# Five idle products among TensorE's first work, and a new order of all work, in a delta-rule attention and cosine-gate kernel

## The chip, the cores and the metric

The kernel runs on one core of a Trainium2 chip. A core has five engines with queues of their own: TensorE (PE in the profile; its weight loads are PEld), VectorE (DVE), ScalarE (ACT), GpSimd (POOL) and SyncE (SP, which here only issues DMAs). Each works through its own list of instructions in order, and waits on semaphores for what others make. The metric is the device time of one execution in microseconds (us); lower is better.

## The reference

```python
q, k, v: (4, 8, 768, 48); beta: (4, 8, 768)           # B, H, S, D
k_n = k / (norm(k) + 1e-06)
for t in range(S):
    y[:, :, t] = q_t @ state
    v_old = k_t @ state
    state = state + beta_t * outer(k_t, v_t - v_old)   # delta rule, state 48 x 48 per head
x = y.transpose(0, 2, 1, 3).reshape(3072, 384)
h = x @ w_in                                           # w_in (384, 2048)
out = (h * cos(h)) @ w_out                             # w_out (2048, 384)
```

The weights arrive in 64-bit words and are narrowed on the chip to 32 bits.

## The kernel before

**Attention.** The sequence is cut into 24 units of 32 steps. All 32 pairs of batch and head of a unit are worked at once. For unit n: `turn` (L589) transposes k and q on TensorE through p_t (from unit 8 on VectorE does it, `turn_blocks`), ScalarE copies them out (`turn_out`, L599), `gram` (L620) makes the products of keys with keys and queries in p_g, and VectorE scales them out (`gram_keys` L634, `gram_queries` L743). The unit's lower triangle has to be inverted. Units 0 to 3 do it by halves: TensorE spreads rows (`rows`, L702, p_r), VectorE (units 0 and 1) or GpSimd (2 and 3) eliminates them (`eliminate`, L722 and L729), `unfold` (L737) lays the result out, and three products solve (`solve_half` and `between`, L859, `solve`, L892). Units 4 to 23 are inverted in pairs on GpSimd (`invert`, L792 and L799, in tiles gb and z), with a trip through DRAM on either side (`gram_put` L761, `gram_get` L770, `put` L803, `get` L812 into zt), and then solve (L892). `solve_out` (L902) scales the solution, `update` (L915) and `update_out` (L923, L925) carry the state on, `state` (L829) and `within` (L932) make the output in p_kq, and `features` (L951) transposes it into x.

**Feed-forward.** Two units make a pair p, 256 tokens. Pairs 0 and 1 multiply x by w_in plainly (`hidden`, L975, p_h, 24 instructions a tile); later pairs use a scheme with fewer products of sums of blocks (`x_sum` L1068, `in_sums` L1115, `layer` L1153, `layer_out`). The gate is h cos h by ScalarE and VectorE (L1016, L1023, L1032, L1035). The output of pair 0 is plain (`output`, L1176), that of the others a seven-product scheme (`product`, L1233, p_out; `left` L1249, `right` L1262, `collect` L1285).

**Weights.** 28 loads (`weights`, L484; 12 for w_in, 16 for w_out) go into six stages that are used in turn, and each is narrowed by ScalarE (`split`, L492 and L494), VectorE (`shift`, L498 and L503) and GpSimd (`add`, L507). A load waits until the sixth load before it is added.

**The order.** The kernel adds 2143 tasks with `add`, each with a key, an engine and what it needs. `Order.LINE` is a written list of all task numbers; `Order.run` (its `run` walks that list) emits the tasks in this order, and so fixes each engine's queue. `Order.OTHER` is a set of tasks that go to their second engine: `x_sum` is GpSimd's unless it is listed, then VectorE's; `left` and `right` are VectorE's unless listed, then GpSimd's; `fold` and `unfold` VectorE's unless listed, then ScalarE's. PSUM has one bank pair for "two" (p_t, p_w, p_v, p_u, p_s, p_z and most p_g), one for p_kq, three banks "h" for p_r and p_h, and p_out. `halfpi` is a column of constants that GpSimd sets at the start.

Of the kernel before, what the change touches and what calls it, by code (L numbers as in the profile page):

```python
# [45 lines left out]

class Order:
# [3 lines left out]
        ('weigh', 1, 0), ('fold', 2), ('weigh', 1, 1), ('fold', 3), ('unfold', 2),  # L51
        ('right', 4, 6), ('x_sum', 2, 'd'), ('x_sum', 2, 'n'), ('x_sum', 2, 'm'),
        ('x_sum', 2, 'e'), ('x_sum', 2, 'k'), ('x_sum', 2, 'g'), ('x_sum', 2, 'i'),
        ('x_sum', 2, 'l'), ('x_sum', 2, 'f'), ('x_sum', 2, 'h'), ('x_sum', 2, 'b0'),
        ('left', 2, 4, 0), ('x_sum', 3, 'd'), ('x_sum', 3, 'n'), ('x_sum', 3, 'm'),
        ('x_sum', 3, 'e'), ('x_sum', 3, 'k'), ('x_sum', 3, 'g'), ('x_sum', 3, 'i'),
        ('x_sum', 3, 'l'), ('x_sum', 3, 'f'), ('left', 3, 4, 0), ('x_sum', 4, 'd'),
        ('x_sum', 4, 'n'), ('x_sum', 4, 'm'), ('x_sum', 4, 'e'), ('x_sum', 4, 'k'),
        ('x_sum', 4, 'l'), ('x_sum', 4, 'h'), ('x_sum', 4, 'b0'), ('left', 4, 1, 0),
        ('left', 4, 4, 1), ('left', 4, 3, 1), ('x_sum', 5, 'd'), ('x_sum', 5, 'n'),  # L60
        ('x_sum', 5, 'm'), ('x_sum', 5, 'e'), ('left', 5, 1, 0), ('left', 5, 1, 1),
        ('left', 5, 4, 0), ('left', 5, 3, 0), ('left', 5, 3, 1), ('x_sum', 6, 'd'),
        ('x_sum', 6, 'm'), ('x_sum', 6, 'e'), ('x_sum', 6, 'g'), ('x_sum', 6, 'i'),
        ('x_sum', 6, 'l'), ('x_sum', 6, 'f'), ('x_sum', 6, 'b0'), ('left', 6, 1, 1),
        ('left', 6, 3, 0), ('left', 6, 3, 1), ('x_sum', 7, 'd'), ('x_sum', 7, 'n'),
        ('x_sum', 7, 'm'), ('x_sum', 7, 'e'), ('x_sum', 7, 'g'), ('x_sum', 7, 'i'),
        ('x_sum', 7, 'l'), ('x_sum', 7, 'b0'), ('left', 7, 1, 1), ('left', 7, 4, 0),
        ('left', 7, 3, 0), ('left', 7, 3, 1), ('x_sum', 8, 'd'), ('x_sum', 8, 'm'),
        ('x_sum', 8, 'k'), ('x_sum', 8, 'g'), ('x_sum', 8, 'h'), ('x_sum', 8, 'b0'),
        ('left', 8, 1, 0), ('left', 8, 3, 0), ('x_sum', 9, 'd'), ('x_sum', 9, 'm'),  # L70
        ('x_sum', 9, 'e'), ('x_sum', 9, 'k'), ('x_sum', 9, 'g'), ('x_sum', 9, 'i'),
        ('x_sum', 9, 'l'), ('x_sum', 9, 'f'), ('left', 9, 1, 0), ('left', 9, 4, 0),
        ('left', 9, 4, 1), ('x_sum', 10, 'd'), ('x_sum', 10, 'n'), ('x_sum', 10, 'e'),
        ('x_sum', 10, 'k'), ('x_sum', 10, 'g'), ('x_sum', 10, 'l'), ('x_sum', 10, 'f'),
        ('x_sum', 10, 'h'), ('x_sum', 10, 'b0'), ('left', 10, 1, 1), ('left', 10, 2, 1),
        ('left', 10, 4, 0), ('left', 10, 3, 0), ('x_sum', 11, 'n'), ('x_sum', 11, 'k'),
        ('x_sum', 11, 'l'), ('x_sum', 11, 'f'), ('x_sum', 11, 'h'), ('left', 11, 2, 1),
        ('left', 11, 4, 0), ('left', 11, 4, 1), ('left', 11, 3, 0),
# [3 lines left out]
9 92 2031 0 1 123 15 2035 16 93 17 2 14 3 11 21 54 55 10 18 2039 56 4 124 60 22 23 57 58 19 20 6 95  # L82
24 181 207 61 26 27 62 53 2043 2047 30 96 32 28 126 29 63 36 65 2032 2036 64 127 25 31 34 33 66 39
2033 35 101 97 2040 67 102 73 132 37 68 40 128 2041 38 98 2037 133 69 184 185 129 2034 2042 41 2038
42 43 44 71 2044 2048 70 8 2051 182 45 46 2045 47 2055 48 49 50 2056 190 78 191 2049 72 51 2052 52
94 7 74 2057 125 2059 103 2060 2063 104 75 105 134 2053 135 137 106 186 2046 2061 138 107 59 2050
131 2058 76 208 2064 108 139 2067 77 2071 2054 237 79 136 2075 183 2065 739 2062 140 141 150 142 740
80 144 81 82 99 741 145 100 147 5 83 143 263 293 2079 84 146 148 153 85 151 86 88 87 210 2068 149 89
2076 742 211 2069 743 12 154 2072 152 744 187 90 156 2066 91 745 240 157 155 2077 109 192 158 159
110 746 193 194 241 130 160 2083 2087 238 759 162 2080 2073 212 2084 213 2081 163 747 760 161 2070  # L90
214 761 164 165 749 195 166 748 2085 2088 111 2078 2082 112 2074 242 215 209 750 217 762 2086 751
763 113 114 2089 752 2091 216 2095 769 115 2092 264 2099 2103 753 2093 116 770 774 117 2100 119 771
243 2101 2107 118 764 772 2096 244 218 120 2108 2094 246 219 247 775 2104 167 121 2090 122 773 168
776 779 777 2097 220 2098 169 2102 221 170 171 2111 807 778 2109 222 319 2115 2105 172 13 2106 173
2119 822 808 809 174 2110 810 175 765 239 2123 177 766 811 767 265 823 2112 295 2116 189 768 349
2127 2131 176 178 817 179 824 2113 818 819 180 820 2124 2120 821 812 266 754 2117 825 267 2121 223
2114 197 826 2125 2118 791 813 755 248 2128 756 296 198 2122 2126 814 249 250 780 268 301 2135 2132
757 815 269 270 2139 827 816 251 271 2129 224 2133 225 2136 272 2140 828 273 2137 792 781 795 2130
758 842 837 302 196 829 830 796 831 838 375 321 322 226 2141 832 2134 880 799 878 879 188 2138 297
2142 199 839 200 245 782 201 203 783 840 843 298 202 785 844 800 888 841 274 803 845 204 205 227 786  # L100
833 882 885 303 793 797 206 228 787 275 229 894 883 323 881 834 230 784 358 294 788 835 836 231 405
233 232 846 789 234 276 847 889 848 235 850 351 236 253 851 304 357 277 900 907 853 854 377 320 902
901 804 352 852 849 910 903 911 305 904 278 306 915 916 906 912 324 802 905 325 856 917 919 326 920
884 908 913 914 254 918 858 859 327 279 307 790 860 890 359 886 909 280 300 926 928 861 895 892 921
929 862 281 801 927 930 932 857 329 922 805 923 891 328 864 252 931 933 924 353 893 330 255 934 925
431 936 866 256 806 935 938 798 939 257 887 937 259 958 260 282 378 867 942 940 258 855 896 354 299
959 954 943 283 284 261 946 868 955 262 960 865 956 285 941 869 331 870 944 794 286 961 945 962 379
287 289 290 288 871 948 963 899 291 309 292 897 898 949 360 863 461 957 1013 952 964 332 950 333 872
361 1015 965 1014 953 874 875 1020 407 1024 362 355 947 1016 1028 380 1017 978 1025 966 1018 350 414
1026 876 951 381 873 1029 376 1019 382 1021 967 363 1030 383 434 1027 968 334 969 1032 1031 335 408  # L110
970 1033 983 979 336 1022 982 337 384 308 1034 985 877 971 310 988 1041 1039 989 1023 972 984 1042
1045 980 981 973 991 385 1035 974 1040 1036 1046 413 1043 975 409 311 1049 1037 976 1038 993 1044
312 977 1047 990 386 1048 1050 986 994 313 315 487 433 987 316 338 992 1051 1055 995 1052 314 415
317 339 469 318 1067 1056 1053 340 1071 996 341 1057 997 1054 342 1068 343 1058 356 345 999 346 344
1001 1061 1072 1002 1063 410 1062 435 1003 1004 347 1069 348 1073 998 1126 1065 416 470 387 406 388
517 543 389 390 1066 1059 1005 1070 417 1064 418 1127 1128 436 463 1075 419 1074 411 437 1060 1076
1129 1137 1006 1141 365 464 1007 391 1138 1142 1133 1130 392 1134 1132 471 1131 1009 1077 1145 1139
439 1146 1079 1000 438 1135 366 1078 1080 1143 1154 1010 1011 393 441 1140 1083 1144 440 1136 465
1084 1081 1155 364 1147 1095 367 1158 1085 1082 466 368 1086 1091 490 1008 489 394 1152 1098 1159
1092 1153 1093 369 371 1156 370 442 1094 525 372 1087 1148 432 1157 526 1162 373 1096 1149 1160 1088  # L120
395 1101 1150 1151 1089 374 1161 396 1102 1163 491 1164 397 1168 1104 398 1165 399 401 1106 1090
1097 1169 402 1184 400 546 573 1166 1172 1167 1185 1188 403 443 1170 1099 404 1171 421 472 412 444
1239 1107 1174 1176 1186 445 1100 1173 422 1240 473 474 527 1108 1187 1109 492 493 1192 1105 1177
545 1110 446 1012 1175 462 1112 1114 447 1178 448 1193 1179 1189 1111 1115 495 475 449 1116 1250
1246 1117 1241 1190 1103 1194 1191 1118 1242 1204 1119 1254 1113 1205 494 519 1251 1247 1120 1243
581 1255 1122 496 1206 420 1248 497 1245 520 1256 1258 423 1123 1195 424 425 427 1180 1259 1124 1207
426 1249 1244 1181 428 1252 1209 1253 1257 1267 1182 1200 1268 451 1260 1201 429 1271 1265 1183 452
# [89 lines left out]
def kernel(  # L217
# [32 lines left out]
    nc = tc.nc  # L250
# [1060 lines left out]
    add = order.add  # L1311
# [498 lines left out]
```

## Time and profile before

| | before |
|---|---|
| three runs, median | 650.61 us (649.26 to 652.42) |
| profiled execution, its time | 650.96 us |
| its span, first to last instruction | 648.2 us |
| mean granted TensorE clock | 0.991 |
| busy: PE, PEld, DVE, ACT, POOL | 618.3, 579.9, 501.3, 264.4, 430.7 us |
| DMA | 49.99 MB, mean 77 GB/s |
| instructions | 28202 |

The profile is of one execution. Busy time counts an instruction from its start to its end; matmuls overlap, and their ends are modelled. The row "PEclk" gives the clock that TensorE was granted, as a share of full speed. The chain that ended last is followed back from the last instruction: each piece was released by the one before it. "issue" is time in which an engine waited for nothing that the profile shows.

The order of TensorE's first tasks in the kernel before, with the start of each in us: turn 0 (4.6), turn 1 (8.4), gram 0 (10.5), gram 1 (13.6), rows of unit 0 (14.7 to 21.3), turn 2, rows, turn 3, rows, solve_half 0 (29.3), between 0 (31.5), rows(1,1) (32.9), solve 0 (36.0), update 0 (38.7), within 0 (40.2), turn 4 (41.7), state 1 (43.2), features 0 (47.1), gram 2 (48.5), rows(1,3) (49.6), gram 3 (51.0), hidden(0,0) (52.1), rows, solve_half 1 (58.4), between 1 (60.1), solve 1 (61.7), update 1 (64.6), within 1 (65.5), turn 5 (68.2), hidden(0,2) (69.1).

### The profile page before, as it was taken

Reading aid. Unit: us, or ns where it says so; the run is one execution under the profiler, and the core shown is the slowest. Engines: PE = TensorE matmul, PEld = TensorE weight load, DVE = VectorE, ACT = ScalarE, POOL = GpSimd, SP = SyncE. Lnnn points to the kernel's source line nnn. Section 1 sums busy time; section 2 is a strip of 40 time slices with the busy share of each in tenths; the row PEclk is TensorE's granted clock in tenths of the full one; section 3 lists DMA queues with packets and bytes.
Section 4 is the critical chain, followed back from the end, with each engine's and each line's share of the span. In section 5 each row is a group of like instructions: output and inputs, shape, how many; then the busy total and the mean of one; then the engine's idle time right before and its main releaser. Section 6 shows DMA issues by size and latency. Waiting matters only on the chain.

```text
span 648.2 us, 28202 instructions
## 1 busy us (share of the span) xinstructions
PE 618.3 (95%) x12306; PEld 579.9 (89%) x12306; DVE 501.3 (77%) x967; ACT 264.4 (41%) x466; POOL 430.7 (66%) x772
## 2 busy tenths in 40 slices
PE   4869899999999989999999999999999999999997
PEld 3858888886899979999999999899999999999997
DVE  7986777899989868788788875788677678757671
ACT  4534655722233432442533532543532434345430
POOL 3446788988858788587787687886786685111211
PEclk9997999999999999999999999999999999999999
DMA  8792475554352544554514443504513302000000
GB/s 163 193 238 66 109 185 139 132 98 78 55 104 41 104 73 62 102 70 76 106 34 71 82 73 70 86 10 62 110 17 69 66 2 43 19 3 25 2 25 24
DMA packets 202923, 49.99 MB, mean 77 GB/s; under 512 B 194544, under 2 KB 197760, under 8 KB 202800
## 3 DMA queue, kind: packets, MB, share of 16 engines
q1 hardware_dynamic: 201536, 47.82, 37.5%
q8 instruction: 96, 1.57, 1.0%
q10 hardware_dynamic: 1088, 0.20, 0.2%
q14 instruction: 27, 0.22, 0.1%
q0 software_dynamic: 176, 0.18, 0.1%
HBM read 38.19 MB, written 9.96 MB: 74 GB/s over the span
## 4 chain that ended last, share of the span: by engine, by line
PE 81%; DVE 6%; DMA 5%; issue 3%; POOL 2%; ACT 1%; SPq 1%; ACTq 0%; DVEq 0%; POOLq 0%
PE p_out L1233 27%; PE p_h L1153 26%; PE p_kq L829 4%; PE p_h L975 3%; PE p_s L915 3%; PE p_r L702 3%; PE p_u L892 3%; PE p_g L620 3%; PE p_kq L932 3%; PE p_out L1176 3%; PE p_o L1233 2%; DMA kp<-in_k_dram 1%; DMA z_dr<-z 1%; PE p_z L951 1%; PE p_t L589 1%
## 5 line engine op out<-in xcount | busy, mean ns | idle before, releaser
L792 POOL TENSOR_TENSOR part<-z,gb 128x126 f32<-128x126 f32 (+22 forms) x310 | 139.9, 451 | 34.9 <-DMA gb<-g_dr 12.5
L799 POOL TENSOR_TENSOR z<-z,part 128x126 f32<-128x126 f32 (+22 forms) x310 | 139.3, 449 | 24.3
L1233 PE MATMUL p_out<-w_out,g_ffn 128*128 128x192 f32 x672 | 123.0, 330 | 0.3 <-DVE o L1285 0.3
L1233 PEld LDWEIGHTS p_out<-w_out,g_ffn 128*128 128x128 f32 x672 | 107.7, 190 | 1.9 <-DVE o L1285 0.5
L1032 ACT ACTIVATE turns<-turns,halfpi 128x512 f32<-128x512 f32 x96 | 68.2, 720 | 63.8 <-DVE turns L1023 63.7
L1233 PE MATMUL p_out<-w_sum,g_ffn 128*128 128x192 f32 x496 | 89.2, 328 | 0.0
L1249 POOL TENSOR_TENSOR g_ffn<-g_ffn 128x512 f32<-128x512 f32 x30 | 41.2, 1380 | 70.1 <-DVE g_ffn L1249 29.2
L1153 PE MATMUL p_h<-x_sum,w_in 128*128 128x128 f32 x640 | 84.0, 278 | 1.5 <-ACT p_h L1165 1.2
L1153 PEld LDWEIGHTS p_h<-x_sum,w_in 128*128 128x128 f32 x640 | 78.2, 191 | 3.3 <-ACT p_h L1165 1.4
L1233 PEld LDWEIGHTS p_out<-w_sum,g_ffn 128*128 128x128 f32 x496 | 79.6, 190 | 0.9 <-issue 0.2
L1016 ACT ACTIVATE turns<-g_ffn,quarter_turn 128x512 int32<-128x512 f32 x70 | 50.4, 721 | 58.5 <-DVE g_ffn L1170 29.7
L1170 DVE TENSOR_TENSOR g_ffn<-g_ffn,p_h 128x512 f32<-128x512 f32 x80 | 54.1, 681 | 18.5 <-PE p_h L1153 14.0
L1023 DVE SCALAR_TENSOR_TENSOR turns<-g_ffn,turns 128x512 f32<-128x512 f32 x70 | 52.8, 760 | 11.6 <-ACT turns L1016 11.4
L1035 DVE TENSOR_TENSOR g_ffn<-turns,g_ffn 128x512 f32<-128x512 f32 x70 | 52.7, 758 | 11.1 <-ACT turns L1032 11.1
L1285 DVE SCALAR_TENSOR_TENSOR o<-p_out,o 128x192 f32<-128x192 f32 x74 | 25.2, 353 | 36.4 <-PE p_out L1233 32.8
L1153 PE MATMUL p_h<-x_sum,in_sum 128*128 128x128 f32 x400 | 52.4, 277 | 0.0
L1153 PEld LDWEIGHTS p_h<-x_sum,in_sum 128*128 128x128 f32 x400 | 49.2, 192 | 0.5
L975 PE MATMUL p_h<-x_ffn,w_in 128*128 128x128 f32 x384 | 48.4, 285 | 0.2 <-issue 0.2
L975 PEld LDWEIGHTS p_h<-x_ffn,w_in 128*128 128x128 f32 x384 | 46.2, 199 | 1.3 <-issue 0.5
L1249 DVE TENSOR_TENSOR g_ffn<-g_ffn 128x512 f32<-128x512 f32 x58 | 43.9, 765 | 3.4 <-POOL g_ffn L1249 2.3
L536 POOL TENSOR_TENSOR knrm<-ksum,halves 128x16 f32<-128x16 f32 (+1 forms) x14 | 36.8, 2629 | 13.4 <-DVE ksum L524 13.4
L1165 ACT COPY p_h<-p_h 128x512 f32<-128x512 f32 x40 | 23.0, 576 | 48.7 <-PE p_h L1153 46.3
(144 smaller groups left out, 1058.1 us busy)
## 6 DMA issues: line engine op xcount, KB each, us to landing
gb<-g_dr SPq DMA_DIRECT2D x20, 256.0 KB, 4.4
vp<-in_v_dram SPq DMA_DIRECT2D x96, 48.0 KB, 3.0
in_sum<-in_moe_w_out_dram SPq DMA_DIRECT2D x12, 384.0 KB, 3.7
out_dram<-o SPq DMA_DIRECT2D x23, 192.0 KB, 2.5
in_sum<-in_moe_w_in_dram SPq DMA_DIRECT2D x8, 512.0 KB, 4.2
kp<-in_k_dram SPq DMA_DIRECT2D x128, 24.0 KB, 1.9
z_dr<-z SPq DMA_DIRECT2D x10, 256.0 KB, 3.6
zt<-z_dr SPq DMA_DIRECT2D x80, 32.0 KB, 2.1
```

The source lines that it names most:

```text
L536: nc.gpsimd.tensor_tensor(out=scales[m][2][:, part], in0=sums[m, part.start][:, 0:n], in1=halves[:, 0:n], op=ALU.pow,)
L792: nc.gpsimd.tensor_tensor(out=part, in0=z[:, 0:rows, j, None].to_broadcast(shape), in1=a[:, j, None, j + 1 :].to_broadcast(shape), op=ALU. ...
L799: nc.gpsimd.tensor_tensor(out=behind, in0=behind, in1=part, op=ALU.subtract)
L975: nc.tensor.matmul(p_h[:, i], w_in[:, t, (4 * k + i) * 128 : (4 * k + i + 1) * 128], xts[p][:, t, unit * 128 : (unit + 1) * 128], start=(i ...
L1016: nc.scalar.activation(turns[p, f], hidden_of(p, f), AF.Identity, bias=quarter_turn, scale=TURN)
L1023: nc.vector.scalar_tensor_tensor(out=r, in0=hidden_of(p, f), scalar=TURN, in1=t, op0=ALU.mult, op1=ALU.subtract,)
L1032: nc.scalar.activation(r, r, AF.Sin, bias=halfpi, scale=2.0 * math.pi)
L1035: nc.vector.tensor_tensor(out=place(p, f), in0=step_of(rests.pop((p, f)), f), in1=step_of(hidden_of(p, f), f), op=ALU.mult,)
L1153: nc.tensor.matmul(p_h[:, e], in_block(*w)[:, e], x_of(p, b), start=new and e == 0, stop=True, skip_group_check=True,)
L1170: nc.vector.tensor_tensor(out=part_of(p, to), in0=part_of(p, one), in1=part_of(p, two), op=op)
L1233: nc.tensor.matmul(p_o, left(p, part, a)[:, e % 4], right(e, b), start=(e == 0), stop=(e == FT // 2 - 1), skip_group_check=True,)
L1249: either(("left", p, x, s), nc.vector, nc.gpsimd).tensor_tensor(out=left(p, s, to), in0=left(p, s, one), in1=left(p, s, two), op=op)
```

## The change

Five tasks ("heat", 0) to ("heat", 4) are added to TensorE. Each multiplies a 128 x 128 operand, the constant column `halfpi` repeated 128 times, with the same column repeated 512, 256, 256, 512 or 128 times, into p_out. Nothing reads the result: the first output product of pair 0 starts p_out anew, and is made to come after the five in the written order. The five depend on no other task.

```diff
+HEAT = (512, 256, 256, 512, 128,)
...
+    def heat(width):
+        one = halfpi.to_broadcast([128, 512])
+        nc.tensor.matmul(
+            flat_out[:, 0:width], one[:, 0:128], one[:, 0:width],
+            start=True, stop=True, skip_group_check=True,
+        )
...
                 if last:
                     deps.append(last)
+                else:
+                    deps += [("heat", x) for x in range(len(HEAT))]
...
+    for i, width in enumerate(HEAT):
+        add(("heat", i), "PE", 0.2, lambda width=width: heat(width))
```

`LINE` is written anew, from

```diff
-9 92 2031 0 1 123 15 2035 16 93 17 2 14 3 11 21 54 55 10 18 2039 56 4 124 60 22 23 57 58 19 20 6 95
+92 0 1 2 21 15 3 16 9 54 2143 10 11 17 55 18 93 123 2031 124 2035 14 4 60 56 57 6 22 2039 95 23 61
```

to its end (2143 to 2147 are the five products). Read out as queues, TensorE's first tasks become: turn 0, **heat 0**, turn 1, gram 0, gram 1, rows(0,0), turn 2, rows(0,1), rows(0,2), state 0, rows(0,3), turn 3, rows(1,2), rows(1,0), solve_half 0, between 0, **heat 1**, solve 0, rows(1,1), update 0, within 0, **heat 2**, turn 4, state 1, features 0, rows(1,3), gram 2, **heat 3**, gram 3, hidden(0,0), rows(2,0), solve_half 1, rows(2,1), between 1, rows(2,2), rows(2,4), solve 1, **heat 4**, rows(2,3), update 1, within 1, turn 5, hidden(0,2). State 0 issues no instruction.

VectorE's queue, from the elimination of unit 0 to gram_keys 2, has in both kernels the same tasks but one (spread(0,1) comes later) in another order; sum(2,0) moves behind solve_out 0, and shift 0 and sum(1,1) behind the last elimination of unit 0. On SP the first loads were k 2, weights 0, k 3, weights 1, q 2, v 0, weights 2, q 3, and are now k 2, q 2, k 3, weights 0, q 3, weights 1, v 0, weights 2. On ScalarE turn_out 3 now stands ahead of unfold 0 instead of behind it. On GpSimd eight instead of ten weight adds stand between the first and the last step of the first inverse (units 4 and 5).

`OTHER` gets a new list, from 117 to 120 entries: 22 left sums and 18 x sums go from VectorE to GpSimd, 15 left sums and 14 x sums the other way; one right sum each way; one fold goes to VectorE, and one unfold to ScalarE:

```diff
-        ('weigh', 1, 0), ('fold', 2), ('weigh', 1, 1), ('fold', 3), ('unfold', 2),
-        ('right', 4, 6), ('x_sum', 2, 'd'), ('x_sum', 2, 'n'), ('x_sum', 2, 'm'),
+        ('weigh', 1, 0), ('fold', 2), ('weigh', 1, 1), ('unfold', 2), ('unfold', 3),
+        ('right', 4, 0), ('left', 1, 2, 0), ('x_sum', 2, 'd'), ('x_sum', 2, 'n'),
...
```

## The prediction

> **What bounds the kernel now.** I read the page first, then stretches of the span with their busy time, then the chain that ended last, the timeline of the first 75 us and the waits. All times are from the one profiled execution: span 648.2 us, time 650.96 us, which is 0.35 us above the median of the three times shown (650.61).
>
> The page's first two parts:
>
> ```profile
> PE 618.3 (95%) x12306; PEld 579.9 (89%) x12306; DVE 501.3 (77%) x967; ACT 264.4 (41%) x466; POOL 430.7 (66%) x772
> ...
> PEclk9997999999999999999999999999999999999999
> ```
>
> TensorE is the engine to watch, and the granted clock shows one dip, at 48.6 to 64.8 us. Stretches of 3.4 us around it (columns: PE, PEld, DVE, ACT, POOL busy with counts, granted clock, DMA share, GB/s):
>
> ```profile
> 39.45:42.80 3.35, 3.35 (x93) 3.01 (x87) 2.43 (x6) 1.00 (x3) 2.23 (x3) 1.00 0.85 276
> 42.90:46.20 3.30, 1.33 (x89) 1.03 (x87) 3.02 (x9) 2.63 (x5) 1.84 (x2) 1.00 1.12 302
> 46.30:49.60 3.30, 2.73 (x110) 2.07 (x110) 2.21 (x9) 1.61 (x3) 0.81 (x1) 0.50 0.71 188
> 49.70:53.00 3.30, 3.30 (x75) 3.11 (x75) 2.46 (x6) 0.25 (x1) 1.68 (x2) 0.50 0.05 10
> 53.10:56.40 3.30, 3.30 (x18) 3.30 (x17) 3.20 (x8) 2.06 (x6) 2.34 (x3) 0.50 0.45 161
> 56.60:59.90 3.30, 3.30 (x81) 2.98 (x80) 3.20 (x9) 2.32 (x5) 1.07 (x2) 1.00 0.18 34
> ...
> 68.00:648.20 580.20, 568.10 (x11201) 535.36 (x11201) 448.16 (x821) 235.77 (x409) 396.07 (x731) 1.00 0.36 67
> ```
>
> The last line says that from 68 us on TensorE works 568.1 of 580.2 us at full clock, so little is to be had there. The others say that a stretch with 40% work (42.9 to 46.2) is followed by half clock, and that this ends after a stretch of unbroken streaming (53.1 to 56.4). From the chain, whole run:
>
> ```profile
> 40.30 1.43 PE p_kq L932 x64
> 41.73 1.58 PE p_t L589 x8
> 44.23 2.07 issue
> 49.70 1.38 PE p_r L702 x6
> 52.20 4.95 PE p_h L975 x24
> 57.14 1.31 PE p_r L702 x8
> 66.33 1.60 issue
> 69.23 2.68 PE p_h L975 x24
> ```
>
> The same 24 products p_h take 4.95 us at 52 and 2.68 us at 69. And the clock row misleads before 42.8 us: it says 1.00, but 64 products p_kq take 1.43 us at 40.30 and 62 take 0.81 us at 65.5, and four transposes begin 213 ns apart at 4.6 and about 110 ns apart at 68. So I read half clock from the start to 42.8 us, full to 46.3, half to 56.5, full after. Up to 29 us that costs little: VectorE has 13.05 us of work in the 15.4 us from 12.0 to 27.4, and its elimination of unit 0's rows ends at 27.4. After that VectorE waits for TensorE:
>
> ```profile
> 37.57 1.02 DVE L902 TENSOR_TENSOR u<-p_u,bz 128x384 f32<-128x384 f32 x2 [1.25 <-PE p_u L892]
> ...
> 40.41 0.96 DVE L925 COPY st<-p_s 128x768 f32<-128x768 f32 x1 [0.89 <-PE p_s L915]
> ...
> 49.74 0.42 DVE L634 TENSOR_TENSOR rows<-p_g,bs 128x256 f32<-128x256 f32 x1 [1.03 <-PE p_g L620]
> ```
>
> **The change, part by part.** *The five products.* 512+256+256+512+128 = 1664 columns. No row shows such a product. The nearest, p_out of 192 columns, does four in 1.30 us, 1.69 ns a column: 2.8 us for all five at full clock, 5.6 at half. They wait for nothing but a constant that is there at 0.8 us; what is queued behind them is the next product on TensorE. Places: heat 0 before the second unit's transposes, in front of a 1.94 us wait of p_g (until 13.58) that nothing here ends sooner; heat 1 while VectorE makes solve(0)'s right side; heat 2 ahead of turn(4); heat 3 before gram(3), whose bank VectorE has first to empty; heat 4 (0.2 us) in the 0.59 us wait of update(1). I take 0 for them: each lies before a wait or beside VectorE. Bounds: 0 and 5.6 us, the latter if the waits are gone and the clock is low; less than nothing is the next item.
>
> *The clock.* From solve(0) to heat 3 the new order leaves TensorE about 14 us of work at half clock (1.48+1.96+1.56+1.43+0.85+1.58+1.7+0.84+1.38+1.19, the chain's rows, heats 1 and 2 and the state product by the above) with no wait I can see before VectorE's gram_keys(2). One stretch like 53.1 to 56.4 is in it, so I expect full clock by about 39 us and no fall at 46. What half clock costs on the chain: from 29.3 to 42.8 p_w 0.73, p_v 0.69, p_r 0.98, p_u 0.60, p_s 0.67, p_kq 0.62, p_t 0.55, 4.8 us in all (each row less the same row after 57 us, p_r halved); from 46.3 to 57.1 p_kq 0.37, p_z 0.51, p_g 0.39 and 0.31, p_r 0.69, p_h 2.27, 4.5 us in all. [...]
>
> *The order of the start.* solve(0) now stands ahead of rows(1,1), which held TensorE from 32.9 to 36.0 while its right side was ready at 34.0. VectorE's waits of 1.25 and 0.89 us go: 2.1 us, at either clock. With full clock the 1.03 us go too, then gram(3) starts when its bank is empty instead of behind p_r (0.45) and runs faster (0.31), and the first hidden tile saves 2.27: 4.1 us. Sum at the end of that tile: 6.2 us (2.6 with a low clock). VectorE is late next: its queue has the same work before gram_keys(2) but spread(0,1). On SP two q loads (4 issues, 1.9 us each) pass weights 0 and 1; their first use is a shift that VectorE does after its elimination, at 27.6 or later, so I cost that at 0, at most 1.9.
>
> *The rest.* Relative order hardly differs. 22 left sums and 18 x sums go from VectorE to GpSimd, 15 and 14 come back: net 7 at 1.27 and 4 at 0.46 us, 11 us more GpSimd of 431. What matters is the inverse on GpSimd: solve(6), (8), (12) and (19) start within 0.9 us of their zt's landing. By summed durations solve(6) stands 1.7 us nearer in TensorE work while GpSimd's weight adds before inverse 3 are the same 28: 1.7 us lost there. The 8.4 us of other idle gaps after 68 us I leave as they are; bounds from 3 us better (the 1.57 at 240 and 1.23 at 407 us gone) to the 7 us of the second rival.
>
> Sum: 650.96 - 6.2 + 1.7 = 646.5; against the median, 646.1.
>
> **Rivals.** *1. The clock falls back.* GpSimd and VectorE pace the start, TensorE at full clock finishes its 14 us early, stands before gram_keys(2) and drops to half as at 46.3. For it: 40% work was enough for that. Against: heat 3 fills 0.85 us there, and 7.45 of 10.2 us busy (59.9 to 70.1) kept the clock. Then 2.6 us are gained, heats 2 and 3 lie open at half clock (2.6): 651.
>
> *2. Slower: the inverse chain.* GpSimd is busy 61.3 of 72 us from 58 to 130, partly by adds that wait for weights. If inverse 3 still starts at 140, whatever the start gained ends in waits of solve(6) for zt, and the later pairs follow: from the second gram to the solve, units 16 and 18 come 0.5 and 5.3 us nearer, units 20 and 22 have 6.9 and 3.0 us more GpSimd work inside their inverse; less the present slack of 1.8, 2.3, 1.1 and 2.7 us and 3.9 us more distance at unit 20, that is 3.0+1.9+0.3, and 1.7 at unit 6: 7 us. Time 657.5. It decides where p_u's waits for zt, now 0.7 us in all, pass 6 us. Against: inverse 2 has two adds less inside (2.6 us).
>
> *3. Full clock from 12 us.* Transposes, heat 0, transposes and gram(0) run without a break from 6.8 to 12.3 us, and the clock stays. All 9.4 us and the 2.07 us gap go, less 1.7: 640.8. Against: VectorE's 13.05 of 15.4 us; TensorE busy without a break from 18.9 to 25.8, with transposes and p_r, did not raise the clock. [...] Unbroken work with transposes before 42.8 did end in full clock, so the trace leaves it open.
>
> **Chances.** Forecast 0.45 (643 to 650), rival 1 0.24, rival 2 0.20, rival 3 0.11. A measurement tells about 0.5%, 3.25 us, from no change, so faster means under 647.4 and slower over 653.9: faster 0.49 (three quarters of the forecast's 0.45, rival 3, a little of rival 1), slower 0.20, same 0.31. Range 639.5 to 657.5: rival 3 to rival 2, as both signs are open.
>
> **What would show it.** Right: p_h's first 24 products take about 2.7 us and end near 51; 64 products p_kq of within(0) take under 1 us, or those of within(1) begin at about 59; no clock of 0.5 after 46. Order: solve_out(0) starts at or before 36.5 without a wait. Wrong: p_g of unit 3 still at 51; heats ahead of an idle VectorE; p_u waiting for zt several us; busy TensorE from 68 us to the end below 97%. Where fetch gaps ("issue", 2.07 and 1.60 us) fall in the new order I cannot tell; one more or less moves the time by 2 us.

## The result, and the profile after

The changed kernel takes 644.8 us (median of four runs, 644.34 to 645.68), beside 650.58 us (649.26 to 652.42) for the kernel before on the same chip: a ratio of 0.9911, 95% interval 0.9884 to 0.9937. By the bound of 0.5% that the prediction set it is faster, and the number is near the forecast of 646.1. The way to it is another than the forecast's. The profiled execution took 644.59 us, its span is 642.8 us (before 648.2), its mean clock by the records 0.981 (before 0.991).

The changed kernel's lines stand 5 (at its start) to 13 (from the output products on) lower in the code: `hidden` is L980 for L975, `state` L834 for L829, `rows` L707, `eliminate` L727 and L734, `collect` L1298, the five products L1194.

From its page, the busy times and the clock row:

```profile
PE 613.6 (95%) x12316; PEld 572.7 (89%) x12316; DVE 505.4 (79%) x955; ACT 263.3 (41%) x467; POOL 447.9 (70%) x783
...
PEclk9677999999999999999999999999999999999999
```

The row shows three low slices of 16 us where it showed one. That is not more half clock: the row of before said full up to 42.8 us, where the prediction read half clock from the products' times (64 p_kq in 1.43 us at 40.30, 62 in 0.81 at 65.5), and this one has records from 12.2 us on. The mean clocks can't be compared for the same reason. GpSimd has 17 us more work (the forecast had 11). The same stretches as in the prediction (PE, PEld, DVE, ACT, POOL busy with counts, granted clock, DMA share, GB/s), the last of them to the new end:

```profile
39.45:42.80 3.35, 2.14 (x52) 1.50 (x52) 3.31 (x7) 0.48 (x1) 3.35 (x2) 1.00 0.88 169
42.90:46.20 3.30, 3.26 (x201) 2.90 (x184) 3.09 (x8) 1.48 (x3) 3.30 (x4) 1.00 0.51 94
46.30:49.60 3.30, 1.03 (x2) 0.20 (x2) 3.20 (x6) 0.00 (x0) 2.34 (x3) 1.00 0.81 241
49.70:53.00 3.30, 1.36 (x65) 1.19 (x65) 2.62 (x13) 1.74 (x5) 0.15 (x1) 0.50 0.93 304
53.10:56.40 3.30, 3.30 (x16) 3.30 (x17) 3.27 (x8) 0.85 (x3) 1.59 (x2) 0.50 0.31 72
56.60:59.90 3.30, 3.30 (x81) 2.78 (x79) 0.56 (x2) 1.14 (x3) 0.84 (x3) 1.00 0.46 136
68.00:642.80 574.80, 565.69 (x11191) 532.84 (x11189) 449.86 (x806) 231.75 (x405) 411.65 (x743) 1.00 0.36 68
```

The clock is full at 39.45, as forecast. Then TensorE works 1.03 of 3.30 us, beside VectorE that works 3.20, and the clock falls to half for the next two stretches. The last line against that of before: TensorE idles 9.1 us after 68 us where it idled 12.1.

The chain of the changed kernel, the pieces that answer to those of before (start, length, what):

```profile
29.47 2.53 POOL w_in L512 x2
...
40.78 0.87 DVE st L930
...
45.58 1.79 DVE in_sum L503
...
47.87 1.28 DVE rows L734
...
51.64 1.34 PE p_g L625 x64
52.98 4.58 PE p_h L980 x24
...
67.90 2.68 PE p_h L980 x24
...
76.72 0.68 issue
```

The first hidden tile (24 products p_h) still takes 4.58 us, at half clock, and ends at 57.57 us; before it ended at 57.14. So nothing of the start's forecast gain is there at this point. VectorE and GpSimd stand on the chain where TensorE stood.

To see where the time is won I compare both traces at equal work: when has TensorE done the same amount of its products, the five new ones not counted? The changed kernel leads by 4.0 us at solve_half 0 (25.36 for 29.33), 0.7 at 43 us, nothing at 64 us, then 1.1 at 77 us, 2.3 at 158, 6.1 at 258, 7.5 at 353, 5.8 at 369 and 5.4 at the end. The start is won early and lost again; four of the 5.4 us come after 77 us. Where the two orders differ such a lead is good to about 1 us. TensorE's waits from 68 to 640 us say what went. First the kernel before (its largest waits), then the changed one (product waiting, what it waited for, total, times, longest):

```profile
PE p_kq L829 <- issue: 2.4, 2, 1.6
PE p_kq L932 <- issue: 1.6, 1, 1.6
PE p_h L1153 <- ACT p_h L1165: 1.2, 1, 1.2
...
PE p_g L620 <- issue: 1.0, 1, 1.0
PE p_g L620 <- DVE tt L743: 0.8, 1, 0.8
PE p_u L892 <- DMA zt<-z_dr: 0.7, 1, 0.7
```

```profile
PE p_out L1246 <- DVE o L1298: 2.2, 2, 1.8
...
PE p_kq L834 <- issue: 1.1, 3, 0.7
...
PE p_h L1158 <- issue: 0.3, 1, 0.3
```

The waits on "issue", on nothing that the profile shows, are most of the difference in these two profiles. From 80 us on they sum to 3.4 us before and 0.8 us after; all other waits listed to 5.1 and 4.0 us, with a new one of 1.8 us in front of an output product.

**The theories.** A: the gain is made before 70 us, by the clock that the five products raise and by solve(0)'s place. B: the start gives nothing lasting, since VectorE is late there, and the gain is made after 70 us by the new order of the rest. Later a third, C: the five products count as instructions, because they move the places where TensorE waits on "issue".

### The profile page after: what moved, and what is told of

It reads as the page before. It is cut to its first block, busy times and chain, and to the rows that moved or that the text cites. A ratio compares the mean times of both kernels' runs of the same rounds, so it can differ in the third digit from the quotient of the medians.

```text
span 642.8 us, 28246 instructions
## 1 busy us (share of the span) xinstructions
PE 613.6 (95%) x12316; PEld 572.7 (89%) x12316; DVE 505.4 (79%) x955; ACT 263.3 (41%) x467; POOL 447.9 (70%) x783
## 4 chain that ended last, share of the span: by engine, by line
PE 87%; DVE 7%; DMA 1%; issue 1%; POOL 1%; ACT 1%; SPq 0%; DVEq 0%; POOLq 0%
PE p_out L1246 29%; PE p_h L1158 28%; PE p_h L980 7%; PE p_kq L834 4%; PE p_out L1181 3%; PE p_u L897 3%; PE p_g L625 3%; PE p_s L920 3%; PE p_kq L937 3%; PE p_o L1246 2%; PE p_z L956 1%; DVE rows L734 1%; PE p_t L594 1%; DVE rows L727 1%; DVE g_ffn L1175 1%
## 5 line engine op out<-in xcount | busy, mean ns | idle before, releaser
L804 POOL TENSOR_TENSOR z<-z,part 128x126 f32<-128x126 f32 (+22 forms) x310 | 145.8, 470 | 24.3
L1246 PE MATMUL p_out<-w_out,g_ffn 128*128 128x192 f32 x672 | 121.6, 329 | 2.0 <-DVE o L1298 1.8
L1262 POOL TENSOR_TENSOR g_ffn<-g_ffn 128x512 f32<-128x512 f32 x37 | 49.0, 1329 | 67.3 <-DVE g_ffn L1040 46.0
L1028 DVE SCALAR_TENSOR_TENSOR turns<-g_ffn,turns 128x512 f32<-128x512 f32 x70 | 55.8, 805 | 15.1 <-ACT turns L1021 14.9
L1040 DVE TENSOR_TENSOR g_ffn<-turns,g_ffn 128x512 f32<-128x512 f32 x70 | 50.9, 736 | 12.7 <-ACT turns L1037 12.6
L1158 PE MATMUL p_h<-x_sum,in_sum 128*128 128x128 f32 x400 | 54.0, 278 | 0.3 <-issue 0.3
L980 PE MATMUL p_h<-x_ffn,w_in 128*128 128x128 f32 x384 | 48.3, 285 | 0.0
L980 PEld LDWEIGHTS p_h<-x_ffn,w_in 128*128 128x128 f32 x384 | 45.7, 198 | 1.0 <-issue 0.2
L541 POOL TENSOR_TENSOR knrm<-ksum,halves 128x16 f32<-128x16 f32 (+1 forms) x14 | 38.8, 2768 | 9.0 <-DVE ksum L529 7.9
L1298 DVE SCALAR_TENSOR_TENSOR o<-p_out,o 128x192 f32<-128x192 f32 x74 | 25.0, 350 | 24.5 <-PE p_out L1246 23.8
```

Source lines behind the costliest of these rows:

```text
L541: nc.gpsimd.tensor_tensor(out=scales[m][2][:, part], in0=sums[m, part.start][:, 0:n], in1=halves[:, 0:n], op=ALU.pow,)
L804: nc.gpsimd.tensor_tensor(out=behind, in0=behind, in1=part, op=ALU.subtract)
L980: nc.tensor.matmul(p_h[:, i], w_in[:, t, (4 * k + i) * 128 : (4 * k + i + 1) * 128], xts[p][:, t, unit * 128 : (unit + 1) * 128], start=(i ...
L1028: nc.vector.scalar_tensor_tensor(out=r, in0=hidden_of(p, f), scalar=TURN, in1=t, op0=ALU.mult, op1=ALU.subtract,)
L1040: nc.vector.tensor_tensor(out=place(p, f), in0=step_of(rests.pop((p, f)), f), in1=step_of(hidden_of(p, f), f), op=ALU.mult,)
L1158: nc.tensor.matmul(p_h[:, e], in_block(*w)[:, e], x_of(p, b), start=new and e == 0, stop=True, skip_group_check=True,)
```

## The experiments

Each kernel was timed against the kernel before on the same chip (its median was 650.97, 650.43 and 650.97 us beside e1 to e4, e5 to e8 and e9 to e11). "Lead at 77 and at the end" compares each profile with that of before at equal work; "issue" and "other" are TensorE's listed waits from 80 us on. They leave out waits on "issue" that end between 74 and 79 us: 2.61 us in e2, 2.42 in e3, 1.81 in e11, 0.7 in the changed kernel and e5, 0.5 in e10.

| kernel | median us | ratio (95%) | span | lead at 77, end | issue | other |
|---|---|---|---|---|---|---|
| changed | 644.8 | 0.9911 (0.9884 to 0.9937) | 642.8 | 1.1, 5.4 | 0.8 | 4.0 |
| e1 no products | 648.08 | 0.9955 (0.9925 to 0.9986) | 646.8 | 2.2, 1.4 | 2.8 | 4.4 |
| e2 old order, products | 650.26 | 0.9996 (0.9970 to 1.0022) | 652.4 | -2.3, -4.2 | 1.4 | 7.0 |
| e3 new start, old rest | 652.16 | 1.0028 (0.9999 to 1.0057) | 652.7 | -1.6, -4.6 | 0.5 | 7.7 |
| e4 old start, new rest | 650.24 | 0.9993 (0.9965 to 1.0020) | 645.8 | -1.2, 2.4 | 2.0 | 3.7 |
| e5 changed again | 646.57 | 0.9920 (0.9892 to 0.9947) | 640.7 | 2.0, 7.5 | 0.2 | 3.9 |
| e6 more products | 643.34 | 0.9888 (0.9859 to 0.9917) | 639.5 | 3.8, 8.7 | 0.8 | 3.0 |
| e7 collect earlier | 641.51 | 0.9855 (0.9828 to 0.9882) | 639.2 | 3.0, 8.9 | 0.4 | 3.8 |
| e8 no adds | 641.03 | 0.9851 (0.9823 to 0.9878) | 640.4 | 6.7, 7.7 | 3.1 | 3.6 |
| e9 tiny products | 645.86 | 0.9915 (0.9885 to 0.9944) | 646.2 | 2.3, 1.9 | 1.1 | 6.6 |
| e10 e6 and e7 | 644.89 | 0.9909 (0.9875 to 0.9943) | 644.0 | 3.4, 4.2 | 4.2 | 3.0 |
| e11 old order, tiny | 651.61 | 1.0021 (0.9996 to 1.0046) | 648.2 | 0.6, 0.0 | 0.5 | 8.4 |

A span is of one execution, and a profiled one can lie 2 to 4 us from its median (e2, e4, e5, e9). The changed kernel itself has leads of 1.1 and 5.4 us in its first profile and of 2.0 and 7.5 in e5. Medians decide on times; profiles only show where a wait is.

**e1: the new order without the five products.** HEAT is empty, and 2143 to 2147 are gone from LINE.

```diff
-HEAT = (512, 256, 256, 512, 128,)
+HEAT = ()
```

> The changed kernel without its five products; the new order is the same. Theory A, which the prediction gave (the gain is made before 70 us, by the earlier clock and by solve(0)'s earlier place): the clock stays at half to about 40 us, the start loses 3 us or more, time 648 to 650 us. Theory B (the gain is made after 70 us, by the order of the rest; in the start VectorE loses the head start to instructions that GpSimd stretches): the time stays within 1.5 us of the changed kernel's 644.8.

648.08 us, ratio 0.9955 (0.9925 to 0.9986): the order alone gives about half of the gain, the products the other half, though the intervals of the two ratios touch. But the half of the products is not made where A puts it: without them the lead at 77 us is 2.2 us, no smaller than with them (1.1, and 2.0 in e5). The clock doesn't need them to rise early either: in e1 it is full from 11.5 to 14.9, 18.4 to 25.2 and 38.8 to 42.3 us, where with them it is full from 12.2 to 22.4 and 39.5 to 49.7.

**e2: the old order with the five products** behind turn 0, between 0, within 0, gram 2 and solve 1.

```diff
+HEAT = (512, 256, 256, 512, 128)
-9 92 2031 0 1 123 15 2035 16 93 17 2 14 3 11 21 54 55 10 18 2039 56 4 124 60 22 23 57 58 19 20 6 95
+9 92 2031 0 1 123 15 2035 16 93 17 2 14 3 11 21 2143 54 55 10 18 2039 56 4 124 60 22 23 57 58 19 20
```

> The kernel before with the five products behind the same tasks as in the change (turn 0, between 0, within 0, gram 2, solve 1), its order kept. Theory A: the clock part of the forecast's sum, 4 us, is gained, 646 to 647 us. Theory B: nothing, 649 to 652 us, as the start is VectorE's and 2.8 us of products do not pay.

650.26 us, ratio 0.9996 (0.9970 to 1.0022): nothing. In this profile the start is 2.3 us behind that of before at 77 us. By themselves the products don't make the start faster, which speaks against A.

**e3 and e4: start and rest exchanged.** In e3 the new LINE and OTHER hold up to hidden(0,2), and the old ones order what is left; e4 is the reverse, without the products. Each has a seam that neither order was made for.

> The changed kernel's order, products and engines up to hidden(0,2) (about 70 us), then the old order and engines for all that is left. Theory A: 645 us, the whole gain. Theory B: 649 to 650 us, the 1.2 us that the changed kernel leads by at 77 us and no more.

> The old order up to hidden(0,2), without the products, then the new order and engines. Theory A: 650 us, as before. Theory B: 645.5 to 647 us, all but the start's 1.2 us; TensorE's idle gaps after 70 us sum to about 5 us instead of 8.4.

652.16 us (1.0028, 0.9999 to 1.0057) and 650.24 us (0.9993, 0.9965 to 1.0020). Neither half gives the gain, and both times are longer than B's (649 to 650 and 645.5 to 647). In e4 TensorE waits 1.46 us for ScalarE until 72.75, in e3 2.42 us on "issue" until 76.72, and half clock follows each (74 to 77.4, 76.8 to 80.2). Whether the wait in e3 is the seam's is not shown: the changed kernel has one of 0.68 us at the same place in TensorE's queue. From 77 us to the end e4 wins 3.6 us on the kernel before, and e3, with the half clock behind its wait, loses 3.0. That fits a gain that belongs to the rest, but the medians of the two don't show it.

**e5: the changed kernel once more**, as the measure for the next three.

> The changed kernel itself, on the chip of the three below, for comparison with them and with the kernel without products (648.1). If the 3.3 us between those two are the products' work, 644 to 645.5 us again. If they are chance (where the clock's 3.4 us stretches fall against TensorE's 1.82 us wait at 350 us, after which the kernel without products got 3.4 us of half clock), the median comes near 647.

646.57 us, ratio 0.9920 (0.9892 to 0.9947), as in the first comparison. The profiled execution (642.47 us) was among its fastest, with 0.2 us of waits on "issue" after 80 us.

**e6: four more products of 512 columns behind the fourth**, ahead of gram 3, where the changed kernel's TensorE waits 4.31 us and the clock falls.

```diff
-HEAT = (512, 256, 256, 512, 128,)
+HEAT = (512, 256, 256, 512, 512, 512, 512, 512, 128)
```

> The changed kernel with four more products of 512 columns behind heat 3, which fill the 4.31 us wait of TensorE before gram(3). Theory A (the clock is on the start's path): the clock does not fall at 49.7, hidden(0,0) takes 2.7 instead of 4.6 us, and the lead stays: 642 to 643 us. Theory B (VectorE paces the start to 67 us): the clock holds, but no more than 0.7 us comes of it.

643.34 us, ratio 0.9888 (0.9859 to 0.9917). The clock no longer falls there, as its stretches show:

```profile
45.00:48.40 3.40, 3.40 (x77) 2.26 (x76) 3.37 (x5) 0.48 (x1) 2.44 (x2) 1.00 0.66 213
48.50:51.90 3.40, 3.40 (x72) 1.58 (x70) 3.02 (x15) 1.21 (x3) 0.78 (x1) 1.00 0.99 270
52.00:55.40 3.40, 3.40 (x28) 3.21 (x28) 3.37 (x9) 1.39 (x5) 1.58 (x2) 1.00 0.59 169
```

The first hidden tile takes 2.94 us there for 4.66, and the lead at 77 us is 3.8 instead of 1.1 to 2.0. So the size that the prediction gave to the clock in this place (2.3 us for the tile) was nearly right, at 1.7; the five products were too few to earn it. The gain over the changed kernel is 1.5 us against its first runs and 3.2 against e5, with intervals that overlap.

**e7: one collect moved up.** In the changed kernel the output product behind the left sums of (4,5) waits 1.82 us at 350.25 for `collect(4,5)`, which stands in VectorE's queue behind two x sums, a right side and a layer's sum. Here it stands right behind layer_out(5,38), eleven tasks earlier.

```diff
-... 1229 1292 1359 1299 1360 ... 478 1290 1295 1230 1231 ...
+... 1229 1292 1230 1359 1299 1360 ... 478 1290 1295 1231 ...
```

> The changed kernel with one VectorE task, the collecting of product 5 of pair 4, ahead of two x sums, a right side and a layer sum instead of behind them; TensorE's p_out waited 1.82 us for it at 348.4 us. If such waits end last, TensorE goes on at once, and the half-clock stretch that can follow the wait is gone: 1.5 to 2.5 us less than the changed kernel. If the time is given back further on, no change.

641.51 us, ratio 0.9855 (0.9828 to 0.9882), the best version that computes the reference; its interval lies below the changed kernel's. The wait is gone, but the gain (3.3 us on the changed kernel, 5.1 on e5) is more than its 1.8 us and than the 1.5 to 2.5 forecast; where the rest comes from stays open. The two lots of output products now follow their neighbours without a break (start, length, product, count):

```profile
342.82 2.77 PE L1336 MATMUL p_out<-w_sum,g_ffn 128*128 128x192 f32 x16
345.42 1.05 PE L1248 MATMUL p_h<-x_sum,in_sum 128*128 128x128 f32 x8
346.31 2.77 PE L1336 MATMUL p_out<-w_out,g_ffn 128*128 128x192 f32 x16
```

**e8: no GpSimd adds for the first eight weights.** The sign and the low bits of most of w_in are left out, so that GpSimd has less to do at the start.

```diff
     def narrow_add(t):
+        if t < 8:
+            words.pop(t)
+            return
```

> The changed kernel without GpSimd's additions of the first eight weight blocks, so that w_in lacks its lowest bits there and the output differs in them. Theory B (VectorE's instructions that run beside GpSimd's are stretched, 8.6 us of it between 25 and 57 us, and VectorE paces the start): the stretch falls under 4 us, gram_keys(2) starts near 46 instead of 50.8 us, and 3 to 5 us stay at the end, 640 to 642 us. Theory A: the start is TensorE's, less than 1 us.

641.03 us, ratio 0.9851 (0.9823 to 0.9878). The stretch from 25 to 57 us, in the kernel before, the changed one and this one:

```profile
25.00:57.00 32.00, 25.14 (x609) 22.64 (x608) 26.48 (x75) 12.88 (x26) 14.73 (x12) 0.84 0.72 197
```

```profile
25.00:57.00 32.00, 21.83 (x596) 18.38 (x597) 29.25 (x68) 12.34 (x25) 19.75 (x15) 0.67 0.79 211
```

```profile
25.00:57.00 32.00, 27.46 (x807) 22.65 (x807) 24.34 (x72) 16.54 (x34) 12.38 (x13) 0.77 0.81 211
```

Third and fifth entries are VectorE and GpSimd. With 5.0 us more GpSimd work VectorE needs 29.25 us for 68 instructions where it needed 26.48 for 75; with the adds away it needs 24.34 for 72. TensorE's waits of 3.61 us before solve(0) and 4.31 us before gram 3 shrink to 0.15 us or nothing, and the lead at 77 us grows from 1.1 to 6.7. Counted over all of VectorE's instructions in this stretch, the excess over the same shape's usual duration is 4.9 us before, 8.6 in the changed kernel and 1.5 here. So it was VectorE, held up by GpSimd, that spent what the new start earned. The rest then gives some back: the lead at the end is 7.7, with 3.1 us of waits on "issue".

**e9: the five products with 8 columns each**, in their places.

```diff
-HEAT = (512, 256, 256, 512, 128,)
+HEAT = (8, 8, 8, 8, 8)
```

> The changed kernel with its five products cut to 8 columns each: they stand in the same places with the same number of TensorE instructions, but stream next to nothing. The changed kernel takes 644.8 us, and without the five products 648.1. If what they give is the clock (half clock from the start until late, heat 0 no longer raises it at 12 us), this one is like the kernel without them, 647 to 649. If what they give is a shift of TensorE's instruction number, by which fewer bursts of small products meet a fetch of instructions (after 100 us the stalls were 1.2 us at 165 and 0.8 at 236 without the products, 0.3 at 367 with them), it is like the changed kernel, 644 to 646, with no stall at 165 and 236 us.

645.86 us, ratio 0.9915 (0.9885 to 0.9944): as the changed kernel, though nearly nothing is streamed. So the streaming of the five is not what makes the difference of about 3 us to e1, as far as runs with these intervals can tell. One sign fits C: e1 and e9 emit the same other products in the same order, and the same burst of products p_g runs in e1 as

```profile
164.12 0.27 PE L715 MATMUL p_g<-kq_t 48*32 48x64 f32 x3
165.56 0.81 PE L715 MATMUL p_g<-kq_t 48*32 48x64 f32 x59 [1.17 <-issue]
```

and in e9, with 20 instructions more ahead of it, as

```profile
163.80 0.92 PE L715 MATMUL p_g<-kq_t 48*32 48x64 f32 x62
```

(start, length, product, count; in brackets the idle time ahead). But e8 has as many instructions on TensorE as e9, in the same order, and stalls all the same, a few products earlier, at the end of the burst p_kq that leads into this one:

```profile
160.08 0.24 PE L927 MATMUL p_kq<-st,kq_t 48*32 48x48 f32 x3 [1.73 <-issue]
```

So the count alone does not decide whether TensorE stalls here. The profiled run of e9 lost the advantage again by waits of 2.35 us (until 168.16, for ScalarE) and 1.81 us (until 354.08) before output products.

**e10: e6 and e7 together.**

> The changed kernel with both edits that helped alone: four more products of 512 columns ahead of gram 3 (643.3) and collect(4,5) right behind the layer_out it stands near (641.5). If the 1.5 us and the 3.3 us are independent, 640; if what is gained at the start is given back at the next wait of the rest, as it was without the adds, 641 to 643. The gap of 1.8 us at 350 should not be there, and the clock should be full from about 44 us on.

644.89 us, ratio 0.9909 (0.9875 to 0.9943): neither 640 nor 641 to 643, and no better than either alone (its interval overlaps both). The clock is full from 40 us on and the collect's wait is gone, as wanted. What stands in their place are waits on "issue", from the list from 68 to 640 us:

```profile
PE p_h L1249 <- issue: 1.6, 2, 1.4
PE p_kq L925 <- issue: 1.5, 3, 0.8
PE p_out L1337 <- issue: 1.2, 1, 1.2
```

**e11: the old order with five products of 8 columns**, in e2's places.

```diff
-HEAT = (512, 256, 256, 512, 128)
+HEAT = (8, 8, 8, 8, 8)
```

> The old order with five products of 8 columns in the places that the full ones had there (650.3 with the full ones, 650.6 with none). If the shift of TensorE's instruction number by some 24 matters by itself, the stalls of 1.0 us at 167, 0.7 at 187 and 1.6 at 242 move or go and the time is 647 to 649. If what stands behind them (a wait for VectorE or GpSimd) takes their place, 650 to 651.

651.61 us, ratio 1.0021 (0.9996 to 1.0046). The stalls at 167, 187 and 242 us are gone and "issue" falls from 3.4 to 0.5 us after 80 us, yet the time doesn't fall. Other waits rise from 5.1 to 8.4 us: the product p_u that follows the vanished stall of 1.57 us waits 1.97 us for zt until 241.86. So at this place the stall lay ahead of a wait that takes over from it. In the old order C gives nothing; that it is a part of the story with the new order of the rest is argued, not shown.

## Why the number was right and the steps were not

The forecast was 646.1 us for 644.8 us. Its largest term, the start, failed, and a term that it left as it was made up for it: that the sum came out near is luck.

**The five products at 0.** Held. They lie in waits or beside VectorE, 5.5 us in all by their rows; and e9, where they stream nothing, is not faster than the changed kernel.

**"Full clock by about 39 us and no fall at 46": half of it.** The clock is full from 39.5 us, but falls at 49.7. That is the fall that rival 1 described, though not its 651 us: TensorE is through with its work at 47.33 and stands 4.31 us before gram 3. Rival 3's condition came too, for a time: the clock is full from 12.2 to 22.4 us (its 9.4 us are the prediction's 4.8 and 4.5 on the chain, added before rounding). Heat 0 was not needed for that rise: in e1, without it, transposes and gram 0 run without a break from 7.52 to 11.7 us and the clock rises at 11.5. What the prediction did not see was that the clock would come early and go again.

**"Sum at the end of the first hidden tile 6.2 us": 0, in the profile -0.4.** The prediction's own sign of being wrong came, "p_g of unit 3 still at 51": it starts at 51.64. Step by step: solve(0) does start earlier, at 33.77 for 36.00, and the solution's scaling at 35.93 for 37.57 (the forecast's "at or before 36.5 without a wait"), so most of the 2.1 us for the place was there at this point. It could have been more, for solve(0) waits 3.61 us for its right side, which stands in VectorE's queue behind three small instructions beside GpSimd's three adds of 29.47 to 33.22 (start, length, line, shape):

```profile
29.50 1.27 DVE L552 TENSOR_TENSOR knrm<-knrm,tiny 128x8 f32<-128x8 f32 x1
30.81 1.20 DVE L554 TENSOR_TENSOR krec<-knrm 128x8 f32<-128x8 f32 x1
...
32.29 0.96 DVE L557 TENSOR_TENSOR bs<-bt,krec 128x8 f32<-128x8 f32 x1
33.17 0.54 DVE L882 TENSOR_TENSOR u_half<-vp,p_v 128x384 f32<-128x384 f32 x1
```

In e8, without the adds, each of the three takes 0.17 us and solve(0) starts at 30.31. One step later the lead is gone: the state's copy starts at 40.70 for 40.41 before, since VectorE has five instructions for weights and sums ahead of it where it had two, and two of the five are stretched (1.14 and 1.05 us for 0.68 and 0.41). The remaining 4.1 us for the clock went at gram 3. "VectorE is late next: its queue has the same work" is the sentence that failed. The tasks up to gram_keys 2 were the same, but their order put more of them ahead of the state's copy, and their duration was not the same. VectorE's instructions from 43.60 us, with GpSimd's below:

```profile
43.60 0.23 DVE L727 TENSOR_TENSOR rows<-rows,p_r 128x72 f32<-128x72 f32 x1
43.86 1.02 DVE L734 TENSOR_TENSOR rows<-rows 128x72 f32<-128x72 f32 x1
...
45.58 1.79 DVE L503 SCALAR_TENSOR_TENSOR in_sum<-in_sum 128x512 uint32<-128x512 uint32 x1
...
47.63 0.20 DVE L727 TENSOR_TENSOR rows<-rows,p_r 128x56 f32<-128x56 f32 x1
47.87 1.27 DVE L734 TENSOR_TENSOR rows<-rows 128x56 f32<-128x56 f32 x1
```

```profile
43.50 1.29 POOL L512 TENSOR_TENSOR w_in<-w_in,w_sum 128x512 uint32<-128x512 uint32 x1
...
45.54 1.29 POOL L512 TENSOR_TENSOR w_in<-w_in,w_sum 128x512 uint32<-128x512 uint32 x1
47.79 1.28 POOL L512 TENSOR_TENSOR w_in<-w_in,in_sum 128x512 uint32<-128x512 uint32 x1 [0.96 <-DVE w_in L508]
```

The subtraction L734, 0.24 us on its neighbours' showing, takes 1.02 and 1.27 us: it ends within 0.1 us of the end of GpSimd's add, at 44.79 and 49.07. L503, 0.68 us alone, takes 1.79 here and ends 0.54 us after the add beside it. The product L727, which reads one operand from PSUM, takes its usual 0.23 us in the middle of the same add. Beside GpSimd's root L541 (27.46 to 29.47, 40.45 to 43.53) L503 took its usual 0.68 us, at 28.38 and at 41.57. But for 0.2 us at 54.81 in the changed kernel, the 4.9 and 8.6 us of excess from 25 to 57 us stand beside a GpSimd instruction, and the excess is 8.6 in e1, e5, e6, e7 and e9 too. That this stretching and GpSimd's own lateness paced the start is shown by e8, which takes away both and doesn't part them.

**"solve(6): 1.7 lost there": not seen.** No product in the changed kernel waits for zt in the list of waits. Rival 2 needed several us of such waits; none came.

**"The 8.4 us of other idle gaps after 68 us I leave as they are": the term that moved.** Listed waits after 80 us fall from 8.5 to 4.8 us. That is 3.7 us, more than the bound of 3 us better. The two gaps named for that bound (240 and 407 us) went, and with them those of 0.97, 0.66 and 0.83 us at 167, 187 and 295 us, while the wait of 1.8 us at 350 is new. What moved most are the waits on "issue", of which the prediction, which calls them fetch gaps, said only that it could not tell where they fall, "one more or less moves the time by 2 us". In these profiles they have a place. Number the records of TensorE's queue in the trace in their order, matmuls, weight loads and the few semaphore instructions among them: the stalls of before come at 46.30 (number 1218), 62.88 (1985), 67.93 (2242), 167.37 (6850), 186.94 (7361, which the profile puts down to zt), 241.62 (9921) and 295.01 us (12482), all 193 or 194 above a multiple of 256, in a burst of small products, and a transfer on the queue q8, of kind "instruction" on the page (96 packets before, for TensorE's 24768 records), starts 2.1 to 2.7 us before each ends. In all thirteen profiles 38 waits of over 0.3 us after 60 us stand at these numbers, two of 256; one on "issue" of that size stands elsewhere (e9, 0.39 us at 136.03). So a kernel whose order or count of instructions is moved by a few has other products at these places. The longest of these waits took 2.6 us (e2, at 78.97).

What makes TensorE stall at one of these numbers and not at another stays open. Nearly all 38 stand in or just behind a burst of small products, but the number does not decide. At number 6850 TensorE, with the same instructions in the same order, waits 1.73 us in e8, 0.21 in the changed kernel and nothing in e5 and e9. And e6 and e10 give it the same instructions too, yet at number 6593 e10 stalls 1.2 us at 161.45 while e6 does not. In e10 the transfer on the instruction queue began only 11 instructions ahead of the place.

**Which part of the gain is whose.** By the ratios the new order alone is 0.45%, 2.9 us of it (e1), and the five add 0.44%, as much again; by e9 they add as much without streaming. That the count of instructions is the cause of that is argued from the moved stalls, not shown: the intervals of e1 and e9 overlap, and e8, with the count of e9, has 3.1 us of waits on "issue". So the cause of the half that comes with the products stays open, and so does what in the order of the rest gives the other half. In e1 there is a second piece: the wait of 1.82 us before the output product, which both kernels have, is followed by half clock. The stretches around it, e1 first, then the changed kernel:

```profile
349.50:352.90 3.40, 1.56 (x11) 1.33 (x11) 3.37 (x7) 0.62 (x1) 1.49 (x3) 1.00 0.82 181
352.90:356.30 3.40, 3.40 (x13) 3.40 (x12) 1.32 (x3) 2.18 (x3) 2.66 (x8) 0.50 0.62 79
```

```profile
346.70:350.00 3.30, 1.73 (x12) 1.29 (x10) 3.27 (x6) 0.62 (x1) 1.92 (x3) 1.00 0.90 197
350.10:353.40 3.30, 3.15 (x21) 3.18 (x22) 2.08 (x6) 2.01 (x3) 2.66 (x7) 1.00 0.63 82
```

After 46% work in a stretch the next was at half clock in e1, after 52% it was not in the changed kernel. The lead falls by 3.5 us in e1 over this place and by 1.7 in the changed kernel: the same wait costs twice as much. Why 52% was enough here and not elsewhere (63% at 19 to 22.3 us was followed by half clock) stays open.

## What to carry to other kernels

When an order is moved, price the instructions of the engine that is late next by what runs beside them: here a subtraction of 0.24 us cost 1.27 beside a GpSimd add, and a start that looked 6 us shorter was not, until the adds were taken away. Waits on "issue" had an address in the instruction stream here (38 of over 0.3 us at two numbers of 256, one elsewhere); list them by number, and over more than one execution, before you credit a reordering or a few extra instructions with the time. And a gain made early counts only as far as the next wait lets it through, so run two good edits together before adding them up: by the medians 1.5 and 3.3 us became nothing in e10.

## What the runs showed of the hardware that was not expected

- TensorE stalled for up to 2.6 us (e2, at 78.97) at instruction numbers 193 or 194 above a multiple of 256, mostly in or just behind a burst of small products, and not each time that the same burst runs over the same number (1.73 us in e8, nothing in e9); 0 to 6.2 us of a profile after 60 us (6.2 before).
- VectorE's subtraction L734, with no input from PSUM, took 1.02 and 1.27 us for 0.24 where a GpSimd add had begun before it, and ended within 0.1 us of the add's end; the product L727, which reads p_r from PSUM, took 0.23 us as usual inside the first of these adds, and beside GpSimd's root L503 took its usual 0.68 us (at 28.38).
- A wait of 1.8 us on TensorE was followed by 3.4 us of half clock in e1 and by none in the changed kernel (46% and 52% work in the stretch around it).
- Between 8.7 and 12.1 us, with heat 0, transposes and gram 0 on TensorE without a break (3.40 of 3.40 us), the clock rises at 12.2 us; in e1, with transposes and gram 0 alone, at 11.5. In the changed kernel it falls again at 22.4 us, behind a stretch of 3.30 us with 2.07 us of work (63%, transposes and rows), where 52% at 346.7 us was not followed by a fall; so the share of busy time alone does not decide.
